# First chunk's inverse copied aside and gated during the second chunk, with another order of loads, in a layer-norm, long-convolution and token-mixing kernel

## The chip, the cores and the metric

The kernel runs on one core of one Trainium2 chip. The metric is the time of one execution in device microseconds, as the median of several runs. The core has five engines that work in parallel, each with its own queue of instructions in program order: TensorE (PE in the profile, its weight loads PEld), VectorE (DVE), ScalarE (ACT), GpSimd (POOL) and SyncE (SP). The kernel's transfers are issued by SyncE and, at the start, by ScalarE; they run on 16 shared DMA engines.

## The reference, cut to what matters

```python
# S, D, F = 2048, 640, 1728
x = A_q
sa, ca, ga, sb, cb, gb = six rows of D of (silu(c) @ w_mod)     # w_mod: 640 x 3840
h = layernorm(x) * (1 + ca) + sa
k_shift = causal depthwise conv of k with shift_k (4 taps)
kv = k_shift * v
y = causal convolution of kv with ssm_k over 2048 tokens, per channel (by FFT of length 4096)
y = y + kv * ssm_D
x = x + ga * (h * y)                                            # the gate
h = layernorm(x) * (1 + cb) + sb
u = gelu(h^T @ w1 + b1); z = u @ w2 + b2                        # mixes tokens, per channel
x = x + gb * z^T
```

## The kernel before, in words

The change lies in the first part, the long convolution with its gate. It works on the 640 channels in NC = 5 chunks of 128 (DC), numbered 0 to 4. The FFT is done with matrix products in two steps forward and two steps back. A chunk goes through these stages; the names are used in what follows.

- **kv operations** (`kv_ops`, recorded at line 59): eight tensor operations per quarter of the tokens make `x`, the product of the shifted k with v: four multiplications with taps, three additions, one multiplication with v into `x`. A quarter runs on VectorE, where the taps and a sum lie in the PSUM tile `tap`, or on GpSimd, where all lies in the SBUF tile `t`. Operations for VectorE are kept in the list `fill`, and `dv(n)` issues the next n at the places where it stands in the code. The taps are copied to `tap` by ScalarE (`taps`, line 170) and to `t` by GpSimd.
- **Forward one** (`step1`, line 219): four blocks of TensorE products for the data (`x`) and four for the filter (`p`), each evacuated by ScalarE into `z` (line 221). The filter comes as ssm_k into `aux` (`load_ks`); GpSimd or VectorE adds D into its first element (`perm_add`, "perm's add"), and ScalarE permutes it into `p` (`perm`, line 164, "the permute").
- **Forward two** (`f2`, line 234): eight groups of TensorE products from `z`. For each group ScalarE copies the filter's half to `kt` (line 238), VectorE makes two products into `p` (the filter's spectrum times the data's), and GpSimd adds them into `y` (two operations per group). `p` and `kt` hold two groups, and TensorE has a ring of three PSUM banks, so it can run three groups ahead of VectorE. The last group's adds run on VectorE.
- **Inverse two** (`i2`, line 263) in two halves from `y`, copied by ScalarE into `z` (line 272), and **inverse one** (`i1`, line 283) in two halves, which needs both halves of inverse two and the constant v1.
- **The gate** (`gate`): ScalarE makes A1 (line 290), the normalized q, row by row (16 of them); VectorE scales and shifts A1 by G1 and G0 (`po`), multiplies it with the inverse's PSUM bank, and GpSimd adds it to x in `xa` or `xb`. `spill` then writes the chunk's columns of x to DRAM.

G0 and G1 come from w_mod by `mod_part` (line 343, five parts), `mod_sum` and `mod_row`. The statistics of q (`bn_stats`, `bn_aggr`) and the root (`rstd`) give the layer norm.

In chunk 0 of the kernel before, SyncE loads q (32 DMAs of 160 KB, line 496) and then w_mod, whose first four parts go to the tiles `v` and `aux`. The inverse's constant v1 shares the tile `v`, and the second ssm_k shares `aux`, so both are loaded behind the products with w_mod. The gate of chunk 0 stands at the end of chunk 0, behind the norm, G0, G1 and inverse one. In chunks 1 to 3 forward one for the next chunk's data is spread between the inverse's halves (lines 591 to 624), and forward one for the next filter comes with and after inverse one.

The order of all work is the order of the code: each engine runs its instructions in the order in which they are written, and waits where an operand isn't there. A DMA also waits for the one issued eight earlier.

## Time and profile before

| | us |
|---|---|
| median of 3 runs | 704.57 (704.09 to 707.8) |
| profiled execution | 707.76 |
| its span, first to last instruction | 706.0 |
| TensorE busy in it | 624.8 (89%) |
| VectorE busy | 485.5 (69%) |
| ScalarE busy | 293.0 (42%) |
| GpSimd busy | 128.3 (18%) |
| start of forward two in chunks 0, 1, 2 | 41.05, 118.86, 168.82 |

A row of the timeline gives the start of a group of like instructions, how long it lasted, its engine, its line, output and inputs by the program's names, shapes and count, and in brackets how long the engine stood idle before it and what released it. TensorE's matmuls of 32-bit floats are counted twice in the trace, since each is run in two passes.

### The profile page before, as it was taken

What the parts mean: (1) busy time and instruction counts of PE and PEld (TensorE: products, weight loads), DVE (VectorE), ACT (ScalarE), POOL (GpSimd) and SP (SyncE); (2) the same over time, 40 slices, a digit from 0 to 9 for tenths busy, and PEclk for the clock granted to TensorE, in tenths of its full rate; (3) what the DMA queues carried; (4) which work ended last, traced back from release to release, by engine and by line L of the source; (5) the groups of instructions that cost most, each with busy time, mean ns of one, the idle gap of its engine ahead of it and who ended that gap; (6) DMA issues with size and microseconds to landing.
All of it is one profiled execution on the core that took longest, in us unless ns stands there. A gap on an engine that the chain in (4) does not pass through costs nothing.

```text
span 706.0 us, 20772 instructions
## 1 busy us (share of the span) xinstructions
PE 624.8 (89%) x9131; PEld 603.1 (85%) x9131; DVE 485.5 (69%) x849; ACT 293.0 (42%) x465; POOL 128.3 (18%) x147
## 2 busy tenths in 40 slices
PE   0698576898999988888799999999999998999997
PEld 0698266888998878778799999999999998999997
DVE  7779338987979539888885213211399959888986
ACT  0444263554746636456666223222335223333331
POOL 5183018512524125000110000000000340000000
PEclk9999888999999999999999999999999999999999
DMA  9977988617343524161303633353163343455411
GB/s 185 248 216 214 368 174 175 149 32 162 71 90 91 172 63 119 58 151 31 59 1 60 118 63 61 75 103 62 53 193 105 106 140 110 145 170 170 148 60 38
DMA packets 167185, 84.91 MB, mean 120 GB/s; under 512 B 89235, under 2 KB 157622, under 8 KB 167094
## 3 DMA queue, kind: packets, MB, share of 16 engines
q1 hardware_dynamic: 162546, 82.27, 46.3%
q10 hardware_dynamic: 4548, 1.31, 1.1%
q8 instruction: 71, 1.16, 0.7%
q14 instruction: 20, 0.16, 0.1%
HBM read 73.07 MB, written 10.49 MB: 118 GB/s over the span
## 4 chain that ended last, share of the span: by engine, by line
PE 64%; DVE 14%; DMA 7%; SPq 5%; ACT 5%; issue 4%; POOL 1%; ACTq 0%; DVEq 0%; POOLq 0%
PE pst L433 21%; PE pst L958 17%; PE pst L1035 7%; PE pst L219 6%; PE pst L263 4%; PE pst L234 4%; SPq L496 3%; PE pst L283 3%; DMA aux<-in_A_ssm_k_dram 2%; DVE p L59 2%; DVE tap L59 2%; DVE kt L59 2%; DMA in<-in_A_k_dram 1%; DMA w<-in_const_w_dram 1%; DMA aux<-in_w_mod_dram 1%
## 5 line engine op out<-in xcount | busy, mean ns | idle before, releaser
L234 PE MATMUL pst<-z,w 128*64 128x64 f32 x2560 | 78.8, 223 | 12.8 <-ACT z L221 5.7
L234 PEld LDWEIGHTS pst<-z,w 128*64 128x64 f32 x2560 | 76.5, 138 | 14.2 <-issue 7.2
L221 ACT ACTIVATE z<-pst 128x1024 f32<-128x1024 f32 x40 | 42.7, 1069 | 52.2 <-PE pst L219 52.1
L219 PE MATMUL pst<-v,x 128*64 128x128 f32 x640 | 40.0, 284 | 26.1 <-DVE x L59 25.2
L59 DVE TENSOR_TENSOR p<-pst,kt 128x512 f32<-128x512 f32 x80 | 51.0, 681 | 15.4 <-ACT kt L238 14.2
L219 PEld LDWEIGHTS pst<-v,x 128*64 128x64 f32 x640 | 37.3, 144 | 28.3 <-POOL t L458 23.4
L59 POOL TENSOR_TENSOR y<-p 128x256 f32<-128x256 f32 x72 | 51.1, 742 | 39.7 <-DVE p L59 39.5
L219 PE MATMUL pst<-v,p 128*64 128x128 f32 x640 | 40.1, 286 | 7.5 <-DVE aux L59 4.8
L831 ACT ACTIVATE pst<-pst,sm 128x640 f32<-128x640 f32 x14 | 10.7, 766 | 86.0 <-PE pst L433 86.0
L219 PEld LDWEIGHTS pst<-v,p 128*64 128x64 f32 x640 | 37.8, 145 | 8.5 <-DVE aux L59 5.0
L958 PE MATMUL pst<-r_z,m_w 128*128 128x320 f32 x222 | 41.6, 309 | 2.2 <-DVE m_w L59 2.2
L238 ACT ACTIVATE kt<-pst 128x512 f32<-128x512 f32 x40 | 23.9, 598 | 44.3 <-PE pst L234 27.5
L263 PEld LDWEIGHTS pst<-v,y 32*128 32x128 f32 x1280 | 38.2, 187 | 3.8 <-issue 2.6
L263 PE MATMUL pst<-v,y 32*128 32x64 f32 x1280 | 40.1, 272 | 0.7 <-ACT z L221 0.6
L946 ACT ACTIVATE m_w<-m_v 128x896 fp32r<-128x896 f32 x24 | 22.7, 951 | 35.1 <-PE pst L958 16.9
L958 PEld LDWEIGHTS pst<-r_z,m_w 128*128 128x128 f32 x222 | 34.8, 188 | 2.4 <-DVE m_w L59 2.4
L59 DVE TENSOR_TENSOR tap<-tap,kt 128x512 f32<-128x512 f32 x51 | 35.5, 696 | 1.3
L59 DVE TENSOR_TENSOR kt<-in,tap 128x512 f32<-128x512 f32 x51 | 34.9, 685 | 1.4
L59 POOL TENSOR_TENSOR m_p<-u_i,r_z 128x320 f32<-128x320 f32 x1 | 0.9, 881 | 188.7 <-issue 188.7
L283 PEld LDWEIGHTS pst<-z,v 64*64 64x64 f32 x1280 | 24.8, 159 | 9.3 <-issue 4.8
L283 PE MATMUL pst<-z,v 64*64 64x64 f32 x1280 | 26.7, 245 | 6.5 <-issue 2.9
L59 DVE TENSOR_TENSOR m_w<-m_v,m_w 128x896 fp32r<-128x896 f32 x24 | 28.1, 1173 | 2.2 <-ACT m_w L946 1.7
(280 smaller groups left out, 1441.7 us busy)
## 6 DMA issues: line engine op xcount, KB each, us to landing
x<-in_B_w_dram SPq DMA_DIRECT2D x22, 512.0 KB
m_v<-in_B_w_dram SPq DMA_DIRECT2D x15, 384.0 KB
x<-in_B_w_dram SPq DMA_DIRECT2D x14, 384.0 KB
aux<-in_A_ssm_k_dram SPq DMA_DIRECT2D x10, 512.0 KB
in<-in_A_k_dram SPq DMA_DIRECT2D x36, 128.0 KB
in<-in_A_v_dram SPq DMA_DIRECT2D x36, 128.0 KB
m_x<-xs SPq DMA_DIRECT2D x28, 160.0 KB
out_dram<-m_x SPq DMA_DIRECT2D x28, 160.0 KB
```

Of the source, the lines that this page charges most:

```text
L59: TT = lambda eng, o, a, b, op: eng.tensor_tensor(o, a, b, op=op)
L219: pe.matmul(ps[64 * ri:64 * ri + 64, o:o + 255:2], lhs, F1[:, 128 * ri:128 * ri + 128], start=True, stop=True)
L221: evac = lambda: act.activation(Z[:, side, t], ps.rearrange("p (a k e) -> p a k e", a=4, e=2), AF.Copy)
L234: pe.matmul(ps[64 * h:64 * h + 64, o:o + 64], W2[k1 // 32][:, 2 * (k1 % 32) + ri], rhs, start=True, stop=True)
L238: act.activation(kt.rearrange("p (m i) -> p m i", i=32), pv[:, :, 1], AF.Copy)
L263: pe.matmul(pp[qd // 2][:, o:o + 64], Y[p, ri, i:i + 2].rearrange("p i k -> p (i k)"), V2[p, 64 * ri:64 * ri + 64], start=ri == 0, stop=ri ...
L283: pe.matmul(ps[64 * b:64 * b + 64, 512 * e + 64 * jj:512 * e + 64 * jj + 64], V1[p, ri, n2], T2[p, :, 32 * ri + n2], start=ri == 0, stop=r ...
L433: pe.matmul(ps[0:m, h, 0:320], w_.bitcast(F32R), r_[:, 320 * h:320 * h + 320].bitcast(F32R), start=first and i == 0, stop=last and i == 2)
L496: sync.dma_start(XH[j // 8][64 * b:64 * b + 64, j % 8], dram(q, (16 * b + j) * D, [[32 * D, 64], [1, D]]))
L946: act.activation(W[n][0].bitcast(F32R), A[p, w_], AF.Copy)
L958: pe.matmul(bank[n], w[:, i].bitcast(F32R), r.bitcast(F32R), start=i == 0 and k == 0, stop=i == 6 and k == 2)
L1035: pe.matmul(acc[s][:, h, 0:320], w[:, f_].bitcast(F32R), u[r + h].bitcast(F32R), start=f_ == 0 and k == 0, stop=f_ == NF - 1 and k == 2)
```

## The change

- **Loads.** The six small loads of b1, b2 and c (tile `g`) move from SyncE to ScalarE's queue. w_mod is loaded ahead of q, into `xa` and `xb`, the tiles of q. Then come v1, the third chunk's taps, and the second ssm_k. q follows once the products with w_mod have read `xa` and `xb`, now in 16 DMAs of 320 KB, and then the third chunk's k and v.
- **First inverse copied aside.** Inverse one of chunk 0 is copied by ScalarE into Y0, the half of `aux` that holds ssm_k. The gate of chunk 0 is done during forward two of chunk 1 in four parts of four rows (`late`): four ScalarE operations, three of VectorE (scale, shift, times Y0) and one add on GpSimd each. Six of the sixteen statistics of q and the root stand there too (the first twelve rows of the list come out ahead of the first product on VectorE).
- **Chunk 1** has a sequence of its own. The kv operations for chunk 2, which stood beside forward two of chunk 1, come after it, one quarter of them on GpSimd; A1 is made after inverse two instead of beside forward two; perm's add, the permute and forward one for the third filter come after the gate, and forward one for the third chunk's data last. Then taps and the kv operations for chunk 3: a quarter on GpSimd, a quarter on VectorE ahead of forward two of chunk 2, two quarters beside it.

The core of the diff:

```diff
+    for h in range(2):
+        act.dma_start(stg[7 * h:7 * h + 6, :], dram(b1, 864 * h, [[128, 6], [1, 128]]))
...
+    def late(n):
+        t = T_t[:, 512 * (n % 2):512 * (n % 2) + 512].rearrange("p (j d) -> p j d", j=4)
+        g = lambda G: G[:, None, 0:DC].to_broadcast([128, 4, DC])
+        x = XH[n // 2][:, 4 * (n % 2):4 * (n % 2) + 4, 0:DC]
+        ac = [lambda j=j: act.activation(t[:, j], XR(4 * n + j, 0, DC), AF.Identity, scale=rs1[:, 4 * n + j:4 * n + j + 1],
+                                         bias=nm1[:, 4 * n + j:4 * n + j + 1]) for j in range(4)]
+        return ac, [lambda: TT(dve, t, t, g(G1), ALU.mult), lambda: TT(dve, t, t, g(G0), ALU.add),
+                    lambda: TT(dve, t, t, Y0[:, 4 * n:4 * n + 4], ALU.mult), lambda: TT(pool, x, x, t, ALU.add)]
...
+            dv(2 if c == 1 else -(-len(fill) // max((6 if c > 2 else 8) - g, 1)))
+            if c == 1 and g == 2:
+                rstd(rs1, nm1, 0, 16)
+            if c == 1 and 2 < g < 7:
+                run(late(g - 3)[0])
+            if c == 1 and g > 3:
+                run(late(g - 4)[1])
...
+        elif c == 1:
+            pool.tensor_scalar(PW, TR.rearrange("p (i s) -> p s i", s=4), 1.0, None, op0=ALU.mult)
+            load_taps(3)
+            run(kv_ops(2, pool))
+            load_ks(2)
+            spill(0)
+            fill.extend(kv(3, ((0,), (1, 2), (3,))))
+            dv(8)
+            i2(0)
+            run(ac[0:8])
+            i2(1)
+            run(ac[8:16])
+            run(po)
+            for half in range(2):
+                ps = i1(half)
+                gate(1, ps, half)
+                dv(2)
+            spill(1)
+            perm_add(2)
+            perm(2)
+            load_ks(3)
+            for t in range(4):
+                step1(1, t)
+            dv(len(fill))
+            for t in range(4):
+                step1(0, t)
+            taps()
+            pool.tensor_scalar(PW, TR.rearrange("p (i s) -> p s i", s=4), 1.0, None, op0=ALU.mult)
+            load_taps(4)
+            run(kv_ops(2, pool))
+            fill.extend(kv(4, ((0,), (1, 2), (3,))))
+            dv(8)
+            continue
...
+            if c == 0:
+                act.activation(Y0[:, 8 * half:8 * half + 8].rearrange("p j (y e c) -> p e (j y) c", e=2, c=2),
+                               ps.rearrange("p (e y c) -> p e y c", e=2, c=2), AF.Copy)
+                continue
```

What this moves on the engines, at three places. First SyncE's queue in chunk 0, before the change, from the first chunk's last small loads on (xa and xb are the tiles of q, in_w_mod is w_mod, in_const_v the constant v1, aux takes ssm_k):

```order
L148 DMA rows<-in_A_shift_k_dram 64x256 x2
L496 DMA xa<-in_A_q_dram 64x640 x16
L496 DMA xb<-in_A_q_dram 64x640 x16
L336 DMA v<-in_w_mod_dram 128x3x640 x2
L336 DMA aux<-in_w_mod_dram 128x3x640 x2
L336 DMA p<-in_w_mod_dram 128x3x640
L560 DMA v<-in_const_v_dram 128x4x1024
L152 DMA aux<-in_A_ssm_k_dram 64x64x32 x2
```

And with the change:

```order
L336 DMA xb<-in_w_mod_dram 128x3x640 x2
L524 DMA xa<-in_w_mod_dram 128x640 x2
L524 DMA xb<-in_w_mod_dram 128x640
L525 DMA v<-in_const_v_dram 128x4x1024
L148 DMA rows<-in_A_shift_k_dram 64x256 x2
L152 DMA aux<-in_A_ssm_k_dram 64x64x32 x2
L155 DMA rows<-in_A_ssm_D_dram 1x64 x2
L497 DMA xa<-in_A_q_dram 64x1280 x8
L497 DMA xb<-in_A_q_dram 64x1280 x8
```

w_mod, the constant and ssm_k have moved from behind q to ahead of it. Next VectorE during forward two of chunk 1, before the change, from the fourth group on (p is a product of the group, tap, kt and x belong to the kv operations):

```order
L59 TENSOR_TENSOR p<-pst_1431,kt 128x512 x2
L59 TENSOR_TENSOR tap<-tap,kt 128x512
L59 TENSOR_TENSOR kt<-in,tap 128x512
L59 TENSOR_TENSOR p<-pst_1476,kt 128x512 x2
L59 TENSOR_TENSOR tap<-tap,kt 128x512
L59 TENSOR_TENSOR x<-tap,in 128x8x32x2
L59 TENSOR_TENSOR p<-pst_1518,kt 128x512 x2
```

And with the change (t is the scratch of a late gate, g holds G0 and G1, aux holds Y0):

```order
L59 TENSOR_TENSOR p<-pst_1341,kt 128x512 x2
L59 TENSOR_TENSOR t<-t,g 128x512 x2
L59 TENSOR_TENSOR t<-t,aux 128x512
L59 TENSOR_TENSOR p<-pst_1383,kt 128x512 x2
L59 TENSOR_TENSOR t<-t,g 128x512 x2
L59 TENSOR_TENSOR t<-t,aux 128x512
L59 TENSOR_TENSOR p<-pst_1429,kt 128x512 x2
```

The late gates have taken the places of the kv operations. Last GpSimd, before the change, from the adds of the gate of chunk 1 on (y adds belong to forward two of chunk 2, aux<-aux,rows is perm's add for the filter of chunk 3):

```order
L59 TENSOR_TENSOR xa<-xa,aux 128x8x128
L59 TENSOR_TENSOR xb<-xb,aux 128x8x128
L59 TENSOR_TENSOR y<-p 128x8x32 x4
L59 TENSOR_TENSOR aux<-aux,rows 1x64 x2
L59 TENSOR_TENSOR y<-p 128x8x32 x10
```

And with the change, from the same adds on (aux<-aux,rows is here perm's add for the filter of chunk 2; t and x are the kv operations for chunk 3):

```order
L59 TENSOR_TENSOR xa<-xa,aux 128x8x128
L59 TENSOR_TENSOR xb<-xb,aux 128x8x128
L59 TENSOR_TENSOR aux<-aux,rows 1x64 x2
L626 TENSOR_SCALAR t<-rows 128x256
L59 TENSOR_TENSOR t<-in,t 128x512 x2
L59 TENSOR_TENSOR t<-t 128x512
L59 TENSOR_TENSOR t<-in,t 128x512
L59 TENSOR_TENSOR t<-t 128x512
L59 TENSOR_TENSOR t<-in,t 128x512
L59 TENSOR_TENSOR t<-t 128x512
L59 TENSOR_TENSOR x<-t,in 128x8x32x2
L59 TENSOR_TENSOR y<-p 128x8x32 x4
```

Perm's add for chunk 2 has moved behind the gate's adds (before, it stood among the y adds of chunk 1), and eight kv operations stand ahead of the y adds of chunk 2.

106 lines of the change are left out of this document (47 added, 59 removed).

## The prediction

> **What bounds the kernel now.** I read the chain of work that ended last first, then TensorE's timeline through the first three chunks, and then the other engines where TensorE waits. Times are us of the profiled span. The page's chain, by engine:
>
> ```profile
> PE 64%; DVE 14%; DMA 7%; SPq 5%; ACT 5%; issue 4%; POOL 1%; ACTq 0%; DVEq 0%; POOLq 0%
> ```
>
> TensorE is the spine, and the change touches only chunks 0 to 2, so I compare arrival times there. TensorE's timeline (start, length, line):
>
> ```profile
> 58.02 7.21 PE L219 MATMUL pst<-v,x 128*64 128x128 f32 x128 [1.82 <-DVE x L59]
> 76.47 3.90 PE L343 MATMUL tap<-v,sm 128*32 128x320 f32 x24 [6.33 <-DMA v<-in_w_mod_dram]
> 81.33 1.28 PE L343 MATMUL tap<-aux,sm 128*32 128x320 f32 x12 [0.97 <-DMA aux<-in_w_mod_dram]
> 85.03 3.80 PE L263 MATMUL pst<-v,y 32*128 32x64 f32 x128
> 102.74 3.71 PE L219 MATMUL pst<-v,p 128*64 128x128 f32 x64 [1.47 <-ACT p L164]
> 111.21 6.49 PE L219 MATMUL pst<-v,p 128*64 128x128 f32 x64 [4.76 <-DVE aux L59]
> 118.86 8.09 PE L234 MATMUL pst<-z,w 128*64 128x64 f32 x269 [1.17 <-ACT z L221]
> 153.50 2.10 PE L283 MATMUL pst<-z,v 64*64 64x64 f32 x128 [0.19 <-ACT z L272]
> 168.82 8.37 PE L234 MATMUL pst<-z,w 128*64 128x64 f32 x263 [1.15 <-ACT z L221]
> 189.18 3.80 PE L263 MATMUL pst<-v,y 32*128 32x64 f32 x128
> ```
>
> Here L219 is forward one (of the data when its input is x, of the filter when it is p), L234 forward two, L263 inverse two, L283 inverse one and L343 the product with w_mod. The reader is to see that the waits between 65 and 119 are for w_mod, which stands behind q on SyncE's queue, and for the first chunk's gate (the wait at 111.21). From 119 on the chunks repeat. I cut the run at three points that the changed kernel has too: the start of chunk 1's forward two (118.86), the moment its product y is complete (141.10), the start of chunk 2's forward two (168.82), and then chunk 2's inverse two (189.18). The windows between them (bounds, length, busy time of PE, PEld, DVE, ACT, POOL, then clock, DMA share, GB/s):
>
> ```profile
> 118.86:141.10 22.24, 19.31 (x572) 18.73 (x574) 19.36 (x33) 12.54 (x26) 12.78 (x17) 1.00 0.68 154
> 141.10:168.82 27.72, 24.02 (x715) 22.24 (x710) 20.75 (x25) 13.64 (x16) 4.75 (x2) 1.00 0.40 75
> 168.82:189.20 20.38, 19.47 (x579) 18.84 (x579) 18.71 (x31) 12.54 (x26) 10.66 (x16) 1.00 0.53 123
> ```
>
> TensorE fills 87%, 87% and 96% of them, and VectorE 87%, 75% and 92%: work added to VectorE in the first or the last has little to hide behind. From chunk 2's inverse two on, every engine has the old order of instructions, so the delay at that point is the whole sum.
>
> **Part 1, the front: the lead.** The second half of forward two's constant lands at 45.40. Large rows move at 402 GB/s:
>
> ```profile
> 36.18 9.22 DMA w<-in_const_w_dram
> 77.00:83.00 6.00, 4.63 (x36) 1.26 (x30) 0.09 (x1) 0.00 (x0) 0.09 (x1) 0.80 1.04 402
> 83.36 16.76 DMA aux<-in_A_ssm_k_dram
> ```
>
> w_mod's 4.9 MB follow it at once and land by 57.6, before TensorE's product at 65.2 (the end of forward one, 58.02 + 7.21); the inverse's constant (2.1 MB) by 62.8. The second ssm_k took 16.8 with that constant ahead of it; even 16.8 more ends at 79.6, and ScalarE permutes it at about 79. q (5.2 MB) may overwrite w_mod from 71.6 and needs 13, to 85; its statistics, twelve at 1.0 on VectorE, end by 93 beside TensorE's work. The third k and v, 18 issues behind q, are needed only at 131. So no load is late: cost 0. The six small loads now stand on ScalarE's queue ahead of the taps and the first permute; they cost ScalarE's queue about 2, which its wait at that place hides: I take 0, bounds 0 and 1.5. The rows of ScalarE and VectorE for this part and the next (start, length of all, instruction, count):
>
> ```profile
> 88.87 2.17 ACT L272 ACTIVATE z<-pst 128x512 f32<-128x512 f32 x4 [2.63 <-PE pst L263]
> 93.03 0.70 ACT L361 ACTIVATE g<-pst 128x640 f32<-128x640 f32 x1
> 102.57 3.17 ACT L290 ACTIVATE aux<-xb,sm 128x128 f32<-128x128 f32 x8
> 117.75 1.06 ACT L221 ACTIVATE z<-pst 128x1024 f32<-128x1024 f32 x1 [1.75 <-PE pst L219]
> 139.10 0.65 ACT L170 ACTIVATE tap<-rows 128x256 f32<-128x256 f32 x1
> 142.58 2.09 ACT L164 ACTIVATE p<-aux 128x2048 f32<-128x2048 f32 x1
> 60.02 0.84 DVE L542 BATCH_NORM_STATS2 sm<-xa 128x6 f32<-128x320 f32 x2
> 111.07 0.69 DVE L59 TENSOR_TENSOR tap<-in,tap 128x512 f32<-128x512 f32 x1
> 121.63 1.29 DVE L59 TENSOR_TENSOR p<-pst,kt 128x512 f32<-128x512 f32 x2 [2.60 <-ACT kt L238]
> 140.03 1.06 DVE L59 TENSOR_TENSOR y<-p 128x256 f32<-128x256 f32 x2
> 145.96 4.60 DVE L59 TENSOR_TENSOR aux<-aux,g 128x2048 f32<-128x2048 f32 x2
> 155.67 1.22 DVE L59 TENSOR_TENSOR aux<-pst,aux 128x1024 f32<-128x1024 f32 x1 [0.17 <-PE pst L283]
> ```
>
> From 65.2: five parts of w_mod, 6.4; inverse two, 3.8; its copies 2.2 and two rows' 1.4, which free its banks (79.0); second half of inverse two, 3.8; copies, 2.2; inverse one, twice 2.1; forward one, 7.2; last copy, 1.1: 97.5, with hand-overs 97.6. The permute lies beside inverse two, the two new copies of the inverse (as a z copy, 1.06) beside TensorE. Forward two of chunk 1 began at 118.86: a **lead of 21.3**.
>
> **Part 2, forward two of chunk 1.** VectorE loses the kv operations for chunk 2 that stood here and gets four statistics of q (1.0 each), the root (1.9 with its wait on ScalarE) and four late gates of three operations. Product 0 starts 2.8 after TensorE (121.63 - 118.86). Then in order: product 1.2, statistics 2.0, product 1.2, statistics 2.0, root 1.9, products 2 and 3 2.4. That is 13.5 from TensorE's start to the first late gate. The late operations read two SBUF tiles, as the old first gate did, with GpSimd beside:
>
> ```profile
> 105.77 4.05 DVE L59 TENSOR_TENSOR aux<-aux,g 128x1024 f32<-128x1024 f32 x2 [1.44 <-ACT aux L290]
> 103.11 1.23 DVE L59 TENSOR_TENSOR aux<-pst,aux 128x1024 f32<-128x1024 f32 x1
> 106.62 2.12 POOL L59 TENSOR_TENSOR t<-t 128x512 f32<-128x512 f32 x1
> 112.38 1.28 POOL L59 TENSOR_TENSOR t<-in,t 128x512 f32<-128x512 f32 x1
> 122.40 1.45 POOL L59 TENSOR_TENSOR y<-p 128x256 f32<-128x256 f32 x2 [1.38 <-DVE p L59]
> ```
>
> The two 128x1024 operations took 2.0 each where one with a PSUM input took 1.23, and GpSimd's beside them 2.12 where it took 1.28 alone: they took turns. So a round is 3 x 0.65 of VectorE and 1.45 + 1.27 of GpSimd (y's two, and the new add into x) in turn, 4.66; the products between stand beside GpSimd. Four rounds less the last add, 17.4, then product 7 and y, 2.3: y is complete 33.1 after TensorE's start (without turns 27.8; as before 22.2 if all hid). I take turns, the nearest row: 33.1 - 22.2 = **10.9 lost**. TensorE is three banks ahead at most and then waits.
>
> **Part 3, the end of chunk 1.** On TensorE the eight blocks of forward one for chunk 2 now stand behind both halves of inverse one, the filter's four first. Those read p, which ScalarE's permute writes, and the permute waits for perm's add of D, which stands on GpSimd's queue behind both adds of the gate. In the old order perm's add came during forward two. So everything hangs on one chain:
>
> ```profile
> 157.04 2.38 POOL L59 TENSOR_TENSOR xa<-xa,aux 128x1024 f32<-128x1024 f32 x1 [17.04 <-DVE aux L59]
> 127.03 0.78 POOL L59 TENSOR_TENSOR aux<-aux,rows 1x64 f32<-1x64 f32 x2
> ```
>
> From y complete: inverse two 3.8; its copies 2.2; eight rows of A1 3.2; the copies of the second inverse two 2.2; eight rows of A1 3.1; scale and shift 4.6; gate 1.2; two kv operations 1.45; gate 1.2; add 2.4; perm's add 0.8; permute 2.1; eight blocks of forward one 14.4 (7.21 for four); last copy of z 1.1; with hand-overs **44.1**, against 27.7 now. TensorE ends inverse one at 15.7 and stands idle until 28.4. VectorE's 24 kv operations end at 33.3, before forward one reads x at 35.7: hidden. Such a pause lowers the clock: after 4.8 idle, two blocks of forward one took 6.49 in place of 3.71 (both quoted above).
>
> ```profile
> 112.00:114.00 2.00, 2.00 (x22) 2.00 (x20) 1.90 (x4) 0.00 (x0) 1.84 (x3) 0.50 0.53 130
> ```
>
> The clock column reads 0.50 in that stretch. I add 2.8 for forward one; inverse two, which also starts after a pause, may lose as much again, which I keep for the range (0 to 2.8), as its work is short. Loss: 46.9 - 27.7 = **19.2**. [...]
>
> **Part 4, forward two of chunk 2** (start S). VectorE's first eight kv operations for chunk 3 wait for taps, which ScalarE copies after the last z: S + 0.7. Ten at 0.725 stand ahead of product 0: S + 7.9. In the old run:
>
> ```profile
> 172.81 1.28 DVE L59 TENSOR_TENSOR p<-pst,kt 128x512 f32<-128x512 f32 x2
> 168.46 2.27 SPq L143 DMA_DIRECT2D in<-in_A_k_dram  x2
> 187.75 1.06 DVE L59 TENSOR_TENSOR y<-p 128x256 f32<-128x256 f32 x2
> ```
>
> that is 4.0 after TensorE. The fourth k and v stand on SyncE's queue behind the second spill, ssm_k and D, and an issue there takes about 1.1 (two in 2.27), so GpSimd's new kv group (8 x 1.34, the 1.28 row and its gap) runs from about S + 2.7 to S + 13.4. The y adds stand behind it, and product 2 needs the first: S + 14.9 (VectorE alone: S + 13.2; bounds 0 and 3.5 later than that). Then a product and two kv operations, 2.65, five times: x complete at S + 28.1; two blocks of forward one 3.7; inverse two at S + 31.9. Now it is 20.4: **11.5 lost**.
>
> **Sum:** -21.3 + 10.9 + 19.2 + 11.5 = **+20.3**. The profiled execution took 707.76 around its span of 706.0: 728.1. It lies 3.2 above the median of 704.57 of the runs shown; on that median the changed kernel takes **724.9, say 725**.
>
> **Rivals.** *Milder, same sign:* no turns (-5.3), the clock stays (-2.8), GpSimd's group in time (-1.7): +10.5, 715. Against it stand the rows where the engines took turns and where the clock fell; for it, that GpSimd was busy only 12.78 of 22.24 in the old stretch and may catch up beside the products. *Not slower:* the chain at the end of chunk 1 hides. Its place is GpSimd's queue, its price 19.2; it decides if the second gate add ends by 15.7 after y, when TensorE ends inverse one, rather than at 25.5. Then -21.3 + 10.9 + 11.5 = +1.1, 705.7; if VectorE's late gates hid as well, -9.8, 694.8. For it speaks only that 16 A1 fit beside forward two in the old run; here they come after. *It does not do what it says:* w_mod or ssm_k land late, as ssm_k's 16.76 warns, and half the lead goes: +31, 735. It decides if the w_mod product waits for a DMA past 65.2.
>
> **Numbers.** Forecast 0.60 (718 to 731); milder 0.20; late loads 0.07; chain hidden 0.06; chain and gates hidden 0.07. The range 713 to 733 leaves the last three out, mostly, and takes in 0 to 1.5 for small loads, 0 to 2.8 for inverse two and 0 to 3.5 for k. Half a per cent, 3.5 us, is about what a measurement of this kernel tells from no change: faster 0.07, same 0.06, slower 0.87.
>
> **What would show it.** Chunk 1's forward two should start near 98; VectorE's t operations should take about 1 us rather than 0.65 and alternate with GpSimd; y complete near 131; TensorE idle some 12 before forward one on p, at a lower clock; chunk 2's forward two near 178 with its first product 8 later. It is wrong if the permute does not wait for GpSimd, or if forward two keeps TensorE's pace of 1.9 per group.

## The result, and the profile after

The changed kernel takes **745.61 us** (median of 4 runs, 744.29 to 748.06) against 705.51 for the kernel before on the same chip (4 runs): a ratio of **1.0568, 95% interval 1.0529 to 1.0606**. The prediction was 724.9, with a range to 733: the sign was right, the size was not. The profiled execution took 744.31 around a span of 742.5, so 36.5 of the 40.1 stand in the two profiles that I compare; the other 3.6 is where those two executions lay among the runs (the one of before 2.3 above this median, the one of after 1.3 below). Ratios here and below are of fast runs alone, since some executions of one kernel take over 1.5% longer than its fastest.

The first thing on the page is TensorE's busy time (us, share of the span, number of instructions) and its clock in 40 slices of the span, here of the changed kernel:

```profile
PE 641.1 (86%) x9131; PEld 622.5 (84%) x9131; DVE 483.0 (65%) x845; ACT 295.3 (40%) x467; POOL 141.6 (19%) x160
...
PEclk9999669656979999999999999999999999999999
```

and the clock of the kernel before:

```profile
PEclk9999888999999999999999999999999999999999
```

TensorE has the same 9131 records of products in both (two to a product of 32-bit floats: 512 in forward two of chunk 1, where the code has 256) and is busy 16.3 longer with them. The clock row goes with that: between 74 and 223 (eight slices of 18.6) it was granted at 5 to 7 tenths in six, where before three slices stood at 8. Then TensorE's timeline of the changed kernel (start, length, line, in brackets the idle time ahead and what ended it):

```profile
39.93 6.63 PE L234 MATMUL pst<-z,w 128*64 128x64 f32 x219 [0.94 <-ACT z L221]
48.54 3.14 PE L234 MATMUL pst<-z,w 128*64 128x64 f32 x101 [1.99 <-issue]
...
54.75 3.89 PE L234 MATMUL pst<-z,w 128*64 128x64 f32 x127 [1.30 <-issue]
60.94 1.32 PE L234 MATMUL pst<-z,w 128*64 128x64 f32 x38 [2.29 <-issue]
...
62.16 4.97 PE L219 MATMUL pst<-v,x 128*64 128x128 f32 x87
...
69.67 2.35 PE L343 MATMUL tap<-xa,sm 128*32 128x320 f32 x24
...
75.18 3.80 PE L263 MATMUL pst<-v,y 32*128 32x64 f32 x128
78.80 3.44 PE L354 MATMUL pst<-kt,sm 1*128 1x320 f32 x9
...
83.04 7.36 PE L263 MATMUL pst<-v,y 32*128 32x64 f32 x124
92.25 4.11 PE L283 MATMUL pst<-z,v 64*64 64x64 f32 x142 [1.85 <-ACT z L272]
99.01 3.46 PE L283 MATMUL pst<-z,v 64*64 64x64 f32 x114 [2.65 <-issue]
102.40 8.24 PE L219 MATMUL pst<-v,p 128*64 128x128 f32 x128
111.77 9.55 PE L234 MATMUL pst<-z,w 128*64 128x64 f32 x320 [1.13 <-ACT z L221]
...
144.04 7.09 PE L263 MATMUL pst<-v,y 32*128 32x64 f32 x124 [0.22 <-POOL y L59]
151.93 7.09 PE L263 MATMUL pst<-v,y 32*128 32x64 f32 x124 [0.81 <-ACT z L272]
160.84 6.28 PE L283 MATMUL pst<-z,v 64*64 64x64 f32 x256 [1.82 <-ACT z L272]
177.63 9.85 PE L219 MATMUL pst<-v,p 128*64 128x128 f32 x128 [10.50 <-ACT p L164]
...
195.60 5.82 PE L234 MATMUL pst<-z,w 128*64 128x64 f32 x192 [1.14 <-ACT z L221]
...
226.23 3.80 PE L263 MATMUL pst<-v,y 32*128 32x64 f32 x128
```

The reader is to see three things. Forward two of chunk 0 is cut by three waits "issue" (5.6 in all), in which the profile shows nothing that was waited for; before it ran through. A fourth such wait, of 2.65, stands inside inverse one (99.01). The same pieces of work take twice as long from 83 on: half of inverse two 7.1 to 7.4 where it takes 3.8 at 75.18. And forward two of chunk 1 starts at 111.77, so the lead is 7.1. Last, the windows of the half rate in chunk 0 and between the points at which the prediction cut the run (inverse two's first product at 143.11 for y):

```profile
80.70:104.60 23.90, 19.41 (x414) 18.30 (x414) 13.14 (x38) 8.49 (x11) 0.00 (x0) 0.50 1.00 209
111.77:143.11 31.34, 16.92 (x512) 16.67 (x513) 27.51 (x47) 12.39 (x26) 17.39 (x19) 0.82 0.01 3
143.11:195.60 52.49, 37.99 (x769) 37.05 (x769) 23.68 (x29) 20.83 (x34) 19.11 (x16) 0.65 0.59 121
195.60:226.23 30.63, 22.99 (x577) 22.60 (x577) 29.38 (x47) 13.08 (x27) 20.18 (x24) 0.83 0.38 87
```

VectorE fills 88%, 45% and 96% of the last three; the granted clock, 1.00 in all three before, is 0.82, 0.65 and 0.83. y is complete at 144.0, when GpSimd's last add releases the rest of inverse two (the row at 144.04), and the parts are:

| | before | after | change | predicted |
|---|---|---|---|---|
| start of forward two, chunk 1 | 118.86 | 111.77 | -7.1 | -21.3 |
| from there to y complete | 22.24 | 32.2 | +10.0 | +10.9 |
| from there to forward two, chunk 2 | 27.72 | 51.6 | +23.9 | +19.2 |
| from there to inverse two, chunk 2 | 20.4 | 30.6 | +10.3 | +11.5 |
| sum | | | +37.1 | +20.3 |

All of the change is made by there. Of the 16.8 that the sum missed, 14.2 lie in the lead and 4.7 in the end of chunk 1; the other two parts came 0.9 and 1.2 lower.

### The profile page after: what moved, and what is told of

Same layout as the page of the kernel before. It is cut to its first block, busy times and chain, and to the rows that moved or that the text cites. A ratio compares the mean times of both kernels' runs of the same rounds, so it can differ in the third digit from the quotient of the medians.

```text
span 742.5 us, 20780 instructions
## 1 busy us (share of the span) xinstructions
PE 641.1 (86%) x9131; PEld 622.5 (84%) x9131; DVE 483.0 (65%) x845; ACT 295.3 (40%) x467; POOL 141.6 (19%) x160
## 3 DMA queue, kind: packets, MB, share of 16 engines
q8 instruction: 71, 1.16, 0.7%
## 4 chain that ended last, share of the span: by engine, by line
PE 57%; DVE 18%; DMA 8%; SPq 5%; ACT 5%; issue 4%; POOL 2%; ACTq 0%; DVEq 0%; POOLq 0%
PE pst L433 20%; PE pst L1002 16%; PE pst L1079 7%; PE pst L263 5%; PE pst L219 4%; DVE p L59 3%; PE pst L283 3%; DMA xb<-in_w_mod_dram 2%; DVE tap L59 2%; PE pst L234 2%; SPq L152 2%; DMA in<-in_A_k_dram 2%; DVE kt L59 2%; DMA xb<-in_A_q_dram 1%; DVE aux L59 1%
## 5 line engine op out<-in xcount | busy, mean ns | idle before, releaser
L234 PE MATMUL pst<-z,w 128*64 128x64 f32 x2560 | 82.3, 229 | 21.3 <-issue 7.2
L234 PEld LDWEIGHTS pst<-z,w 128*64 128x64 f32 x2560 | 80.4, 144 | 23.5 <-issue 13.2
L59 POOL TENSOR_TENSOR y<-p 128x256 f32<-128x256 f32 x72 | 54.2, 783 | 71.9 <-DVE p L59 71.8
L219 PE MATMUL pst<-v,x 128*64 128x128 f32 x640 | 40.1, 286 | 29.8 <-DVE x L59 27.6
L219 PEld LDWEIGHTS pst<-v,x 128*64 128x64 f32 x640 | 37.8, 145 | 30.7 <-POOL aux L59 23.2
L263 PEld LDWEIGHTS pst<-v,y 32*128 32x128 f32 x1280 | 48.4, 228 | 15.2 <-POOL y L59 11.3
L263 PE MATMUL pst<-v,y 32*128 32x64 f32 x1280 | 50.6, 316 | 11.8 <-POOL y L59 11.0
L1002 PEld LDWEIGHTS pst<-r_z,m_w 128*128 128x128 f32 x222 | 34.8, 188 | 2.4 <-DVE m_w L59 2.4
L272 ACT ACTIVATE z<-pst 128x512 f32<-128x512 f32 x38 | 20.6, 635 | 37.9 <-PE pst L263 37.9
L59 DVE TENSOR_TENSOR tap<-tap,kt 128x512 f32<-128x512 f32 x48 | 33.4, 696 | 1.2
L59 DVE TENSOR_TENSOR kt<-in,tap 128x512 f32<-128x512 f32 x48 | 32.9, 686 | 1.5
```

The source lines that it names most:

```text
L59: TT = lambda eng, o, a, b, op: eng.tensor_tensor(o, a, b, op=op)
L219: pe.matmul(ps[64 * ri:64 * ri + 64, o:o + 255:2], lhs, F1[:, 128 * ri:128 * ri + 128], start=True, stop=True)
L234: pe.matmul(ps[64 * h:64 * h + 64, o:o + 64], W2[k1 // 32][:, 2 * (k1 % 32) + ri], rhs, start=True, stop=True)
L263: pe.matmul(pp[qd // 2][:, o:o + 64], Y[p, ri, i:i + 2].rearrange("p i k -> p (i k)"), V2[p, 64 * ri:64 * ri + 64], start=ri == 0, stop=ri ...
L272: act.activation(o, i, AF.Copy)
L1002: pe.matmul(bank[n], w[:, i].bitcast(F32R), r.bitcast(F32R), start=i == 0 and k == 0, stop=i == 6 and k == 2)
```

## The experiments

My theories at this point: (a) TensorE's waits "issue" come from its instructions arriving late while large loads fill the DMA engines; (b) the small loads on ScalarE's queue hold up the start; (c) the clock, at half rate for 24 us in chunk 0 and for 31 and 14 in chunk 1, is on the path; (d) the prediction's own chains for the rest: turns of VectorE and GpSimd, perm's add behind the gate, GpSimd's late kv group. Most of these kernels were run once, and one execution of the changed kernel lies up to 4 from another (of run 11's up to 12), so I judge them by the points in their traces and give the time beside.

**1. The small loads back on SyncE's queue.**

```diff
-    act.dma_start(stg[14:30, :], dram(b2, 0, [[128, 16], [1, 128]]))   # and the other five
...
     sync.dma_start(T_w2[1], c_w2[:, 4096:8192], max_dma_last_dim=4096)
+    sync.dma_start(stg[14:30, :], dram(b2, 0, [[128, 16], [1, 128]]))  # and the other five
```

> The changed kernel with its six small loads (b1, b2, c) back on SyncE's queue, behind the second half of forward two's constant, and the transpose that reads them back behind forward one of chunk 1's data. In the changed kernel forward two of chunk 0 ends at 62.1 and forward two of chunk 1 starts at 111.8. Theory 'small loads': on ScalarE's queue they hold up the loads of k and v for chunk 1 by some 2 us, which comes back through GpSimd's kv operations and VectorE's product 2 (which stands 4.5 idle): forward two of chunk 0 ends 2 to 4.5 earlier, at 58 to 60, chunk 1's forward two starts at 107 to 110, and the time falls by 2 to 4 from 745.6. Rival 'instruction fetch': what stretches forward two of chunk 0 are TensorE's own waits of 2.0, 1.3 and 2.3 that end with no releaser; they stay, chunk 0 ends at 61 to 62 and the time moves by less than 1.5.

Measured: 751.32; forward two of chunk 0 ends at 62.9, chunk 1's starts at 116.6. Theory (b) has half a point: GpSimd's kv group starts at 37.3 in place of 39.6, as in the kernel before. But TensorE still waits 0.8, 2.4 and 0.8 with no releaser, and nothing of that half reaches forward two's end. Then the product with w_mod waits 2.55 for the activation of c, which now comes behind forward one. So the small loads alone are not where the lead went.

**2. A fifth of w_mod.**

```diff
-        mod_load(0, kk, T_x[kk // 2][:, 1920 * (kk % 2):1920 * (kk % 2) + 1920])   # kk = 0 to 3, and three more
+    mod_load(0, 0, T_x[0][:, 0:1920])
+    pl = [pl[0]] * 5
```

> The changed kernel, but only the first of the five parts of w_mod is loaded for the first three rows, and it is used for all five products; this leaves out 3.9 MB of the loads that run between 46 and 58 (and gives other values of scale, shift and gate). All instructions on TensorE, VectorE, ScalarE and GpSimd stay. Theory 'instruction fetch': TensorE's waits with no releaser in forward two of chunk 0 (5.6 us in all) come from its instructions arriving late behind the large rows of w_mod; without them these waits fall below 1.5 us, forward two of chunk 0 ends at 57 to 59 and chunk 1's forward two starts 3 to 5 earlier, at 107 to 109. Rival 'bound by VectorE and GpSimd': the waits go but the end of forward two of chunk 0 moves by less than 1, as products and the adds into y set it. Rival 'TensorE itself': the waits stay at 4 us or more. q's loads stand behind the products in all cases and are not expected to matter.

Measured: 748.15; waits of 1.4 and 1.9, end of forward two at 62.4, chunk 1's at 113.7. This does not tell the theories apart: v1 and ssm_k moved up into w_mod's place, and the DMA engines stayed full to about 57.

**3. All large loads held back.** So the next run holds w_mod, v1, taps and ssm_k behind ScalarE's last kt copy.

```diff
+            act.activation(T_x[0][:, 0:1], epsc, AF.Copy)
+            for kk in range(4):
+                mod_load(0, kk, T_x[kk // 2][:, 1920 * (kk % 2):1920 * (kk % 2) + 1920])
...
             for t in range(4):
                 step1(0, t)
```

> The changed kernel with the loads of w_mod, v1, the taps and the second ssm_k held back until ScalarE has made its last kt copy of chunk 0's forward two (about 61), so that nothing large runs beside forward two of chunk 0; the product with w_mod must then wait for w_mod to about 75, so the whole time is expected to be 5 to 12 longer and only forward two of chunk 0 is looked at. (With a fifth of w_mod the next loads took its place at once, and the DMA engines stayed full until 58.) Theory 'instruction fetch behind large rows': TensorE's waits with no releaser in forward two of chunk 0 (5.6 us in the changed kernel, 0 before) fall below 1, and forward one of chunk 1's data starts at about 60 in place of 62.2; the rest of the lag to the 58.0 of before stays, as GpSimd's kv group still ends 2 later. Rival 'TensorE itself': the waits stay at 3 or more with nothing large on the DMA engines.

Measured: 751.33. TensorE in forward two of chunk 0 of this run:

```profile
42.38 6.75 PE L234 MATMUL pst<-z,w 128*64 128x64 f32 x222 [1.14 <-ACT z L221]
49.45 3.13 PE L234 MATMUL pst<-z,w 128*64 128x64 f32 x98 [0.32 <-issue]
52.82 5.82 PE L234 MATMUL pst<-z,w 128*64 128x64 f32 x192 [0.24 <-DVE p L59]
60.59 8.87 PE L219 MATMUL pst<-v,x 128*64 128x128 f32 x128 [1.95 <-DVE x L59]
```

and the windows of that stretch (second last column the DMA share), in the changed kernel and here:

```profile
46.00:58.00 12.00, 7.94 (x257) 7.56 (x255) 7.14 (x12) 2.23 (x4) 11.23 (x15) 1.00 1.04 396
```

```profile
43.00:59.00 16.00, 15.08 (x500) 14.69 (x494) 11.47 (x19) 4.46 (x8) 15.53 (x18) 1.00 0.27 107
```

The waits fall from 5.6 to 0.3: theory (a) holds, they belong to the full DMA engines. What they cost is less than the stage shows. From forward two's start to forward one of the data it takes 18.2 in place of 22.2 (17.0 before), but forward two also starts 2.4 later here (42.38 against 39.93). Within the span forward one starts at 60.59 in place of 62.16, so **1.6** earlier, where the kernel before has 58.02. VectorE holds the rest: its third product waits for GpSimd's adds, which stand behind a kv group that starts at 39.6 in the changed kernel, at 39.9 here, and at 37.3 before and in run 1. The third product in the changed kernel and here:

```profile
50.92 1.39 DVE L59 TENSOR_TENSOR p<-pst,kt 128x512 f32<-128x512 f32 x2 [4.47 <-POOL y L59]
```

```profile
51.28 1.39 DVE L59 TENSOR_TENSOR p<-pst,kt 128x512 f32<-128x512 f32 x2 [2.38 <-POOL y L59]
```

So two causes lie over each other: with the waits alone (run 1) forward one starts at 62.9, with the late group alone (this run) at 60.6, with neither (before) at 58.0; forward two itself starts between 39.9 and 42.4 in these. At the end of forward one next to nothing is won: it takes 8.87 here, where it took 7.21 before, and ends at 69.5 against 69.7.

That what is late are instructions is read from the trace's DMA packets: the queue "instruction" (q8) moves blocks of 16,384 bytes, and in the changed kernel each wait ends 1.3 to 1.6 after such a block has landed:

```
block starts  lands   TensorE goes on
46.11         47.13   48.54
52.31         53.39   54.75
58.50         59.62   60.94
95.82         97.41   99.01
```

Before, the blocks in this stretch started 3.7 to 4.4 apart; here they come 6.2 apart.

**4. Products that nobody reads, to hold the clock.** First try, written into a spare part of the tile tap:

```diff
+            pe.matmul(tap[:, 896:1024], F1[:, 0:128], F1[:, 128:256], start=True, stop=True)   # n times
```

> The changed kernel with matrix products that nobody reads (128x128 by 128, into a spare part of the PSUM tile tap) where TensorE waits: 16 and 6 between the products for the rows of w_mod, 14 ahead of inverse one of chunk 0; in chunk 1, 75 ahead of inverse two, 5 between its halves, 14 ahead of inverse one and 80 ahead of forward one of the filter. Theory 'clock': TensorE stands at clock 0.5 from 80.7 for 24 us, from 135.3 for 31 and from 169.4 for 14, only because its work there is sparse. With the waits filled the clock is back at 1.0 for most of it; the second half of inverse two of chunk 0 takes 3.8 to 4.5 in place of 7.4, the halves of chunk 1 about 3.8 each in place of 7.1, inverse one of chunk 1 4.2 in place of 6.3, forward one of the filter 7.2 in place of 9.9; chunk 1's forward two starts at 104 to 108 in place of 111.8, from y complete to forward two of chunk 2 takes 44 to 47 in place of 52, and the time falls by 8 to 13 from 745.6. Rival 'chain': the halved rate is hidden behind ScalarE, VectorE and GpSimd, or these small matrix products run slowly for another reason: the time moves by less than 3.

Measured: 783.76. The fillers waited for VectorE's kv operations, which use the same tile, and ran behind them (16.05 idle, then 19.30 of fillers ahead of inverse two). As a test of the worth of the clock the run fails. It does tell the rates: at clock 1.0 the halves of inverse two in chunk 1 take 3.80 each, inverse one 3.96 and forward one of the filter 7.21, in place of 7.1, 7.1, 6.3 and 9.9.

**5. The fillers in the bank that the next product writes anyway.**

```diff
+    def warm(ps, n):
+        for _ in range(n):
+            pe.matmul(ps[0:64, 0:128], F1[:, 0:64], F1[:, 128:256], start=True, stop=True)
...
     def i2(r, eng=None, n=0):
         pp = [psum(), psum()]
+        warm(pp[0], n)
```

> The changed kernel with matrix products that nobody reads (64x128 by 128) put into the bank that the next product writes anyway, so that they wait for nothing else: 16 ahead of the first row of w_mod and 12 ahead of inverse one in chunk 0; in chunk 1, 30 ahead of inverse two, 5 between its halves, 12 ahead of inverse one and 85 ahead of forward one of the filter. (In the first try they wrote into the tile tap and stood behind VectorE's kv operations; that run told the rates at clock 1.0, not what they are worth.) Theory 'clock': the half rate is on the path. In chunk 0 the second half of inverse two takes about 3.8 in place of 7.4 and inverse one gains some 2 more, so chunk 1's forward two starts at 104 to 108 in place of 111.8; from y complete to forward two of chunk 2 takes 43 to 47 in place of 52; the time falls by 9 to 14 from 745.6. Rival 'chain': ScalarE, VectorE and GpSimd set the pace there, and the time moves by less than 4.

Measured: 750.04. A filler took 0.22 and not 0.11, so the 85 ahead of forward one of the filter held it up to 188.4, while its permute had ended at 180.9; chunk 1's forward two started at 116.7. Neither number of the theory came, but the counts were wrong, so it is run again.

**6. The fillers fitted to the waits** (8 and 7 in chunk 0; 40, 3, 7 and 44 in chunk 1).

> As the try before with products that nobody reads, but fitted to the waits. There one of them took 0.22 and not 0.11, so the 85 ahead of forward one of the filter took 18.7 and held it up by 8, and those of chunk 0 overran. Now 8 and 7 in chunk 0, and 40, 3, 7 and 44 in chunk 1. Theory 'clock': both halves of inverse two of chunk 1 take 3.8 in place of 7.1, so ScalarE's A1 rows and all behind them come 5 to 6 earlier, forward one of the filter runs at full rate (7.2 in place of 9.9), and from y complete to forward two of chunk 2 takes 43 to 45 in place of 52; the time falls by 6 to 10 from 745.6 (more, if chunk 0 gains too: forward two of chunk 1 at 108 to 110 in place of 111.8). Rival 'chain of ScalarE, VectorE and GpSimd': not under 49.

Measured: 741.99. From inverse two's first product (144.80) to chunk 2's forward two (193.48) it takes 48.7 in place of 52.5: **3.8 less**, or 47.8 counted from y, under the rival's bound but not the 43 to 45 that the theory wanted. Of the 3.8, 2.6 are forward one of the filter, which takes 7.2 as it should, and 1.2 come from inverse two, as VectorE's scale starts 18.7 after y in place of 19.9. At inverse two of chunk 2 nothing of it is left (226.84 against 226.23). Inverse two shows why no more came (lines are shifted in this kernel: L270 is inverse two):

```profile
145.73 4.88 PE L270 MATMUL pst<-v,y 32*128 32x64 f32 x120 [0.47 <-POOL y L59]
...
152.01 7.11 PE L270 MATMUL pst<-v,y 32*128 32x64 f32 x128
```

```profile
144.80:148.00 3.20, 2.72 (x84) 2.59 (x88) 3.07 (x5) 0.00 (x0) 3.03 (x3) 0.96 0.02 5
148.00:152.00 4.00, 4.00 (x58) 3.56 (x54) 2.78 (x4) 1.38 (x3) 3.84 (x4) 0.50 0.81 147
152.00:159.00 7.00, 7.00 (x129) 6.92 (x128) 0.00 (x0) 3.80 (x10) 5.25 (x5) 0.50 0.87 165
```

TensorE was busy for 2.72 of 3.20 and then for 4.00 of 4.00, and the clock fell to 0.50 at 148 all the same, in the middle of inverse two, and stayed there up to 159, the end of its second half. Its products have 32 rows (32*128 in the timeline). In chunk 0 there was no gain at all: 42.1 from forward one's end to chunk 1's forward two as in the changed kernel, with 5.8 of waits "issue" in place of the 2.65.

**7. Perm's add and the permute ahead of the gate.**

```diff
             run(po)
+            perm_add(2)
+            perm(2)
             for half in range(2):
                 ps = i1(half)
                 gate(1, ps, half)
                 dv(2)
             spill(1)
-            perm_add(2)
-            perm(2)
```

> The changed kernel with perm's add and the permute for the third filter put ahead of the gate of chunk 1 instead of behind it, nothing else. Theory 'chain behind the gate adds' (part 3 of the prediction): TensorE stands idle for 10.5 before forward one of the filter because the permute waits on GpSimd's queue. With the edit forward one of the filter starts right behind inverse one, at about 168 in place of 177.6, and stays in part at clock 1.0; then VectorE's kv operations (end at 182.3) are late next, so forward two of chunk 2 starts at 189.5 to 191.5 in place of 195.6 and the time falls by 4 to 6 from 745.6. Rival: the permute then waits for ssm_k's load or for ScalarE's A1 rows, and TensorE for z, still read by inverse one: the start of forward two of chunk 2 moves by less than 2.

Measured: 739.97. TensorE at that place:

```profile
166.53 2.12 PE L219 MATMUL pst<-v,p 128*64 128x128 f32 x32
...
182.12 8.97 PE L219 MATMUL pst<-v,x 128*64 128x128 f32 x128 [6.44 <-DVE x L59]
192.20 3.02 PE L234 MATMUL pst<-z,w 128*64 128x64 f32 x96 [1.12 <-ACT z L221]
```

The wait for the permute is gone, and VectorE's x is late next, at 182.1, as expected. From inverse two's start (142.74 here) to forward two of chunk 2 takes 49.5 in place of 52.5, so **3.0**, a little less than the 4 to 6 expected: forward one of the data, behind its new wait, runs in part at half rate (8.97 in place of 7.15). At inverse two of chunk 2 1.9 of it is left (224.31 against 226.23).

**8. Two edits in two places.** The late gate's add on VectorE, and the taps ahead of forward one of the data:

```diff
-                    ..., lambda: TT(pool, x, x, t, ALU.add)]
+                    ..., lambda: TT(dve, x, x, t, ALU.add)]
...
             dv(len(fill))
+            taps()
             for t in range(4):
                 step1(0, t)
-            taps()
```

> Two edits in two places of the changed kernel. First, the late gate's add into x goes from GpSimd to VectorE. Theory 'turns' (part 2 of the prediction): without that add GpSimd and VectorE take fewer turns, VectorE's late operations on t fall from 1.0 to 2.0 each to about 0.7, and from the start of forward two of chunk 1 to y complete takes 28 to 30 in place of 32. Rival: VectorE's queue is full there and the added 0.7 four times eats it: 31.5 to 33. Second, the taps for chunk 3 are copied ahead of forward one of chunk 2's data instead of behind it. Theory 'VectorE's eight kv operations hold product 0' (part 4): they end before forward two of chunk 2 starts, product 0 starts 3 to 4 after it in place of 7.7, and inverse two stands 26 to 28 after it in place of 30.6. Rival 'GpSimd's group': its kv operations wait for k's load until about forward two's start, the y adds stand behind them, and product 2 needs the first of these; then inverse two comes 29 to 30.6 after, a gain below 1.6.

Measured: 745.68. VectorE in the first place, then in the second:

```profile
130.11 1.98 DVE L59 TENSOR_TENSOR t<-t,g 128x512 f32<-128x512 f32 x2
132.12 0.69 DVE L59 TENSOR_TENSOR t<-t,aux 128x512 f32<-128x512 f32 x1
```

```profile
193.96 0.70 DVE L59 TENSOR_TENSOR tap<-in,tap 128x512 f32<-128x512 f32 x1 [8.21 <-DMA in<-in_A_k_dram]
...
209.88 1.38 DVE L59 TENSOR_TENSOR p<-pst,kt 128x512 f32<-128x512 f32 x2 [3.51 <-POOL y L59]
```

First place: the third operation falls from 1.1 to 0.69, but scale and shift stay at 0.99 each beside the y adds, and the add is 0.69 more on VectorE. Inverse two starts 34.8 after forward two in place of 31.3: worse even than the rival had it, so the add is better where it was. Second place: inverse two of chunk 2 stands 29.7 after forward two in place of 30.6, 0.9 won, as the rival said. The early taps don't help much: VectorE then waits 8.21 for chunk 3's k, which is issued behind the spill, ssm_k and D, and its third product waits 3.51 for the y adds, which stand behind GpSimd's group (198.5 to 209.1).

**9. Statistics and root ahead of forward two of chunk 1.**

```diff
-            for j in range(10):
+            for j in range(16):
                 q_stats(j)
-            fill.extend(lambda j=j: q_stats(j) for j in range(10, 16))
...
-            if c == 1 and g == 2:
-                rstd(rs1, nm1, 0, 16)      # now behind inverse one of chunk 0
```

> The changed kernel with all sixteen statistics and the root ahead of forward two of chunk 1, where VectorE stands idle for 17 from 97 on, instead of ten there and six, with the root, inside. Theory (part 2 of the prediction): four statistics and the root, 5.9 of VectorE, stand ahead of the first late gate and delay y by as much. Then y is complete 26 to 28.5 after the start of forward two of chunk 1 in place of 32, the start stays at 111 to 113, and the time falls by 4 to 6 from 745.6. Rival 'the late gate waits for its place in the code anyway': it stands behind the fifth group, whose products wait on the y adds and on banks; then y comes 30 to 32 after, and the time falls by less than 2.5.

Measured: 743.94. Forward two of chunk 1 starts at 112.5 and inverse two 27.1 later in place of 31.3, **4.2 less**; the theory holds, at the lower end. Inverse two of chunk 2 comes at 222.5 in place of 226.2. At the end of the span only 0.3 is left; the granted clock of this execution was 0.932 in the mean of its span, against 0.940 in the changed kernel's.

**10. The first gate ahead of forward two again.** The new loads and the inverse copied aside stay (the third chunk's k and v come in another order); chunk 1 has its old sequence.

```diff
+            run(kv_ops(2, pool))
+            run(ac[0:4])
+            dv(8)
             for t in range(4):
                 step1(1, t)
+                run(ac[4 + 2 * t:6 + 2 * t])
+            late(0)                         # half a gate: scale, shift, times Y0, add; the other half behind product 1
-        elif c == 1:                        # chunk 1's own sequence goes
```

> The new order of loads and the inverse copied aside, as in the changed kernel, but with the first gate ahead of chunk 1's forward two as far as it goes: all sixteen statistics, the root and the first half of the gate on VectorE while TensorE does inverse one and forward one of the filter, the second half behind product 1; chunk 1 has the old sequence again (kv operations beside forward two, A1 there, forward one spread between the halves of the inverse). Theory 'the lead is real, the new chunk 1 throws it away': forward two of chunk 1 starts at 111 to 114, takes 24 to 28 to y complete (137 to 141 against 141.1 before), and the time is 700 to 706. Rival 'queue of GpSimd': its kv group for chunk 2 waits for k and v behind q, and the adds of the gate and of y stand behind it; y complete at 143 or later and 708 to 715.

Measured: 710.83. Forward two of chunk 1 starts at 118.9, chunk 2's at 174.3. Its trace shows two waits that I had put there: the root's square root stands on ScalarE behind the copy of the second half of inverse one (VectorE waits 6.2), and the second half's add stands on GpSimd ahead of the y adds (6.6 idle).

**11. The same without these two waits.**

```diff
+                if not half:
+                    rstd(rs1, nm1, 0, 16)   # between the two copies of inverse one
...
+            if c == 1 and g == 3:
+                add()                       # the second half's add, no longer at g == 1
```

> The run with the early gate again, with two waits taken out that its trace showed: the root's square root on ScalarE now stands ahead of the copy of the second half of inverse one (VectorE waited 6.2 for it, and ScalarE's A1 rows and z copies behind it, so that forward two of chunk 1 began at 118.9 and not at 112), and the second half's add on GpSimd stands behind the first y adds instead of ahead of them (6.6 idle). Theory 'the lead is real if nothing is queued behind the late root': forward two of chunk 1 starts at 111 to 114, y is complete 23 to 26 later (135 to 139, against 141.1 before), chunk 2's forward two starts at 162 to 167 against 168.8, and the time is 698 to 704, under both kernels. Rival 'fetch and clock hold the front': it starts at 115 or later and the time is 704 to 711.

Measured: 710.07 (median of 10 runs, 704.38 to 716.09), ratio to the kernel before **1.0046, 95% interval 1.0013 to 1.0079**, so no gain on it. TensorE, in an execution that took 715.59:

```profile
101.31 3.46 PE L283 MATMUL pst<-z,v 64*64 64x64 f32 x114 [3.91 <-issue]
...
115.09 8.00 PE L234 MATMUL pst<-z,w 128*64 128x64 f32 x256 [2.00 <-ACT z L221]
...
189.49 3.80 PE L263 MATMUL pst<-v,y 32*128 32x64 f32 x128
```

The rival had it: instruction waits and clock hold the front, forward two starts at 115.1, and at chunk 2's inverse two all of the lead is gone (189.49 against 189.18 before; of the 7.8 that this execution's span is longer, 7.5 lie behind that point). Still this tells where the loss lies: with the same loads and the inverse copied aside, but the old chunk 1, the kernel is within half a per cent of before. So nearly all of the 36.5 goes with the late gates beside forward two and chunk 1's new sequence, which this run takes away together.

**12. q, k and v held back behind chunk 0's inverse one.** This and the next two were made to settle the front.

```diff
-            load_q()                         # and the third k and v, behind the product with w_mod
...
+                if half:
+                    act.activation(T_x[0][:, 0:1], epsc, AF.Copy)
+                    load_q()                 # and the third k and v
```

> The changed kernel with the loads of q and of the third k and v held back until ScalarE has copied the second half of chunk 0's inverse one aside, so that nothing large runs from 75 on while TensorE does both inverses and forward one of the filter; q then lands after about 120 and everything in chunk 1 is late, so only the start of forward two of chunk 1 is looked at, as the time from the end of forward one of chunk 0's last data product (69.7 in the changed kernel) to it: 42.1 there. Theory 'fetch': the wait of 2.65 in inverse one goes, the work stays at clock 0.5, and it takes 38.5 to 40. Rival 'TensorE waits there for something else': 41.5 to 42.5, with the wait still there.

Measured: 752.86. TensorE from inverse two's second half on:

```profile
82.72 7.26 PE L263 MATMUL pst<-v,y 32*128 32x64 f32 x124
91.81 5.85 PE L283 MATMUL pst<-z,v 64*64 64x64 f32 x256 [1.83 <-ACT z L272]
...
106.82 4.41 PE L234 MATMUL pst<-z,w 128*64 128x64 f32 x142 [1.13 <-ACT z L221]
115.82 2.50 PE L234 MATMUL pst<-z,w 128*64 128x64 f32 x50 [4.59 <-issue]
```

The wait inside inverse one is gone, and from forward one's end (70.0) to forward two takes 36.8 in place of 42.1: **5.3**, more than the wait itself: the half rate also ends 8.5 earlier, at 96.0, within inverse one, which is unbroken here. 0.8 of the 5.3 stands ahead of inverse one. The wait moved with the loads: at 115.8, beside q, stands one of 4.59.

**13. The same with the fillers.**

> As the run with q, k and v held back, and with the 8 and 7 products that nobody reads in chunk 0 (ahead of the first row of w_mod and ahead of inverse one). Theory 'clock as well': without waits for instructions the fillers hold the clock at 1.0, the second half of inverse two takes 3.8 in place of 7.4 and inverse one 4 in place of 7.6, and from the end of forward one to forward two of chunk 1 takes 31 to 35 in place of 42.1 (the prediction had 32.4). Rival 'inverse two is too thin to hold the clock even in unbroken work' (as in chunk 1, where it fell in the middle of it): the second half stays at 6 to 7.4, and it takes 36 to 39.

Measured: 755.36; 37.6 from forward one's end to forward two, and the second half of inverse two still takes 6.6 (84.2 to 90.8). The rival holds: fillers do not bring what the clock takes there.

**14. The edits that helped, together.**

> The edits that helped, together in the changed kernel: all statistics and the root ahead of forward two of chunk 1 (4.2 less to y), perm's add and the permute ahead of the gate (3.0 less to forward two of chunk 2), the taps ahead of forward one of the data (0.9 less), and fillers ahead of inverse two and inverse one of chunk 1 (30 and 7, part of the 3.8 that the fitted fillers gave). If they add up, inverse two of chunk 2 stands at 216 to 219 in place of 226.2 and the time is 8 to 10 below the changed kernel, 735 to 738, still 4 to 5 per cent above the kernel before. If one cause had been counted twice (VectorE's kv operations as the bound of the end of chunk 1 in all of them), it is 739 to 742.

Measured: **736.53 (median of 4 runs), ratio 1.0419, 95% interval 1.0342 to 1.0497**, in the range for pieces that add up. Inverse two of chunk 2 stands at 221.6, later than the 216 to 219 expected, as this execution's forward two of chunk 1 began at 114.4. The fillers ahead of inverse two did not lift its rate here (7.09 for each half). It is still slower than the kernel before, and no version here beats that one.

## Why the prediction missed

**Part 1, the lead: this is the step that failed.** The prediction put chunk 1's forward two at 97.6, the sum of TensorE's work "with hand-overs"; it came at 111.77. The loads were in time, as it said: the product with w_mod waited for no DMA, nor did VectorE for q. It failed in what the loads do to TensorE and in the rate at which TensorE works.
- Ahead of 69.7 it is 4.5 late (predicted 65.2); 4.1 of this stand at the start of forward one already (62.16 against 58.02). "Cost 0" was wrong for the large loads, beside which TensorE's instructions come late (5.6 of waits, run 3), and for the small ones, which were given 0 to 1.5: with them GpSimd's kv group starts 2.3 later (run 1). The two lie over each other. Taking out the waits alone moved forward one's start by 1.6, taking the small loads away alone did not bring it forward (62.9); no run takes out both.
- From there to forward two it takes 42.1 in place of 32.4. By the rows, the second half of inverse two took 3.6 more than its term, inverse one 6.0 more (2.65 of it the wait) and forward one of the filter 1.0 more, and the product with w_mod 0.9 less. Of the 9.7, 5.3 go with the wait inside inverse one and the half rate behind it (run 12). The remaining 4.4 stand in rows at clock 0.5, above all the second half of inverse two (7.36, where I had 3.8); that this half rate is their cause is read from the rows, as the fillers could not lift it (runs 6 and 13).

The prediction used its row at clock 0.50 only behind the long pause in chunk 1. In the front the half rate came without a long pause, at 80.7, as the products for w_mod's rows (one row each, 1*128; 3.44 for nine records of them) came singly; that they wait for banks, which ScalarE's copies of inverse two free, is read from the order of the code and not tested.

**Part 2, forward two of chunk 1: right.** 32.2 against 33.1. The turns are there. VectorE and GpSimd in the first round, with nothing beside VectorE, and in the second, in the changed kernel:

```profile
125.94 1.41 DVE L59 TENSOR_TENSOR t<-t,g 128x512 f32<-128x512 f32 x2
...
129.18 1.99 DVE L59 TENSOR_TENSOR t<-t,g 128x512 f32<-128x512 f32 x2
```

```profile
124.31 1.43 POOL L59 TENSOR_TENSOR y<-p 128x256 f32<-128x256 f32 x2 [1.13 <-DVE p L59]
...
129.44 2.34 POOL L59 TENSOR_TENSOR y<-p 128x256 f32<-128x256 f32 x2
```

VectorE's scale and shift took 1.41 with GpSimd idle and 1.99 with GpSimd's adds beside them; GpSimd's two y adds took 1.43 beside VectorE's products, which read PSUM, and 2.34 beside scale and shift. The statistics and the root, 5.9 in the sum, were worth 4.2 when taken out (run 9).

**Part 3, the end of chunk 1: the mechanism right, one term mis-sized.** The chain through GpSimd's adds, perm's add and the permute is there (10.50 idle ahead of forward one of the filter), and putting perm's add first takes that wait away (run 7). The time is 51.6 in place of 46.9. The clock term for forward one held (2.6 against 2.8); the one for inverse two was mis-sized. I had kept 0 to 2.8 for the range "as its work is short", and nothing in the sum; both halves took 7.1 in place of 3.8. All of the miss stands ahead of VectorE's scale, which starts 19.9 after y, where the sum has 14.5:

```profile
163.85 4.62 DVE L59 TENSOR_TENSOR aux<-aux,g 128x2048 f32<-128x2048 f32 x2 [14.67 <-ACT aux L290]
```

Inverse one took 6.3 in place of 4.2, but ends at 167.1, hidden behind this scale and shift. The fillers won 3.8 in all, 1.2 of it ahead of the scale, with the second half of inverse two still slow (run 6).

**Part 4, forward two of chunk 2: the size right, one wait wrong.** 30.6 against 31.9, the first product 7.7 behind TensorE's start against 7.9. The sum lets product 2, the third, wait for the y adds behind GpSimd's kv group. That wait did not come: the group started at 195.06, 0.5 ahead of forward two and not 2.7 behind it, and product 2 started at 208.38 with VectorE idle nowhere between. VectorE alone sets the pace, as the part "GpSimd's group in time" (1.7) of the rival "milder" had it. Run 8 shows that GpSimd's group comes next: with the taps early, product 2 waits 3.51 for it.

**The rivals.** "Not slower" asked for the second gate add to end by 15.7 after y; it ended at 174.8, 31 after. "Late loads, +31" comes nearest in number, by luck, and has the wrong place: its condition, a product that waits for w_mod's DMA past 65.2, did not come. The clock, which "milder" had staying up, went the other way. The range ended at 733 because it held uncertainty for the clock in one place only and none for TensorE's instructions.

What stays open: whether inverse two could run at full rate in both halves at this place without long fillers ahead; the split of the 4.4 between its rate and the rows of w_mod; and what the front takes with the waits and the late kv group both gone.

## What to carry to other kernels

A load that lands in time is not free: beside w_mod's loads, at a DMA share of 1.04, TensorE waited 5.6 in forward two of chunk 0 here, and 0.3 at a share of 0.27 (run 3). The row to look for is a wait "issue" beside such a share. When a reorder puts thin products or pauses together on TensorE (here the products for w_mod's rows, with 23.9 at clock 0.50 from 80.7, and the 10.77 idle ahead of 143.11, with 30.7 from 135.3), work out the stage at half clock as well as at full clock, and let the range reach to that sum. And a gate or an add moved "beside" another stage has to be counted on the engines that this stage already fills: here VectorE at 87 and 92% left no room.
